# A fused attention and expert kernel on one core: one more token block by seven half-size products, another order of the first loads, another written-out order of the work

## The chip, the core and the metric

The kernel runs on one core of one Trainium2 chip. A core has five engines with queues of their own, each in order: TensorE (PE, the matrix products; its weight loads are listed apart as PEld), VectorE (DVE), ScalarE (ACT), GpSimd (POOL) and SyncE (SP). They wait for each other through semaphores. The metric is the device time of one execution in microseconds (us), the median of the runs.

## The reference

What is computed is an attention with a narrow window, and behind it two matrix products with a squared ReLU between them:

```python
# q, k, v: [8 batches, 8 heads, 576 positions, 64]
scores = q @ k.transpose(0, 1, 3, 2) / 8
scores = where(abs(pos[:, None] - pos[None, :]) <= 32, scores, -1e9)
attn = softmax(scores)
o = attn @ v
x = o.transpose(0, 2, 1, 3).reshape(8 * 576, 512)     # 4608 tokens of 512
h = x @ w_in                                          # 512 x 2048
r = maximum(h, 0.0)
g = r * r
out = g @ w_out                                       # 2048 x 512, float32
```

## The kernel before

**Attention.** The 8 x 576 queries are cut into 24 groups of 192, numbered G (batch `G // 3`, third `G % 3`). For a group the q, k and v rows are loaded; q and k are turned so that the head dimension lies on the partitions; a score step S (lines 600 and 609) multiplies them, an exponential X on ScalarE (627, 630) and, from the second batch on, a mask multiply M on VectorE (635) follow, then the product P with v (665), the reciprocal and the normalisation on VectorE (681, 684), and the turn T of the result into x transposed (`xt`). Most groups do this in two halves, A and B. P B of a group needs the upper half of its accumulator set to zero, which ScalarE does for most groups (656); the groups below `ZG` do without and write P B in 64-column tiles instead, twice as many matmuls.

The first three groups get their mask as a bias added by PE (`NPM = 3`, line 600). Groups of the first two batches are turned by PE (552, 701, 706) and copied out by ScalarE and VectorE (561, 564, 711); the later ones by transposing DMAs on the SP queue (572 for q and k, 715 and 718 for x).

**First product, x @ w_in.** It starts as soon as tokens are there. Up to token 4096 a piece of it, `mm1`, is some matmuls into one 512-wide bank (736: A), a ReLU out of that bank on ScalarE (742) and a square on VectorE (745). Pieces are 192 tokens wide below token 768, 256 below 2048, then 512. The tokens from `512 * MSTART` on take `mm1_strassen` instead. This computes the product of 2 x 2 blocks by seven products of half the size in place of eight, with sums of blocks of x (807, VectorE) and of w_in (792). One round handles a quarter of the hidden columns: 28 matmuls of 256 columns (835), two 512-wide products at a time in two banks, `x` and `y`. Between the seven products ScalarE copies a bank aside three times (842, "seed", `u` and `p`). Two of the four result blocks come straight from a bank (a ReLU on ScalarE, 861, a square on VectorE, 855); the other two are sums of a bank and a copy (`hb`, VectorE, 872), which a letter `ADDED` then sends on: "A" is a ReLU and a square on ScalarE (861, 853), "M" a ReLU on ScalarE and a multiply on VectorE (855), "D" one fused VectorE instruction that takes the maximum with zero and multiplies by the sum. One of the sums of w_in (`sums_w1(..., late=True)`) is written over a part of w_in that a plain `mm1` reads, so it comes behind the last plain piece.

**Second product, g @ w_out.** The first 512 tokens take plain matmuls (756), all others a seven-product form of their own (941 for the matmuls, 954 for copies, 912 for sums of g, 975 to 985 for the output). The last 512 tokens have a variant of it (`last`, 994 to 1024).

**The loads.** q, k and v are float32 in memory and are cast to bfloat16 on the way by DMAs issued from POOL (487 for q and k, 516 for v, 523 and 528 for 512 KB chunks of w_in and w_out). `load_hw` is the other way: a plain DMA issued by SP or ScalarE (503) into a float32 buffer and a cast on VectorE or ScalarE (505). The list `OPEN` gives the loads of the first batch, the engine of each, and a first order.

**What sets the order.** Nothing runs as it stands in the code. Each step is recorded with an estimated duration and a key, `Prog.schedule` simulates the five engines and the DMA queues by these estimates and always takes the ready step with the smallest key, and `emit` writes each engine's steps in the order so found, with waits where a step depends on another engine's. `ADJ` is a list of 1,143 numbers, one per step, added to the keys. Up to the first second-product step the planner fills gaps of PE with small matmuls on zeros (416). On the chip the order is fixed; a step that is late holds up all that stands behind it on its engine.

The kernel's other constants that the change touches: `SEP = (0,)` gives group 0 separate score banks, and `TB` does not exist yet: groups 0 to 2 are all turned in bank `outp0`.

Of the kernel before, what the change touches and what calls it, by code (L numbers as in the profile page):

```python
# [7 lines left out]
BF16 = mybir.dt.bfloat16  # L8
# [15 lines left out]
MSTART = 8  # L24
# [13 lines left out]
NSPLIT = 6  # L38
NXT = 6
DIRECT = "D"  # L40
ADDED = "A"
SEP = (0,)
ZG = 1
ADJ = dict(enumerate((
# [322 lines left out]
class Gen:  # L367
# [217 lines left out]
    def scores(self, G, ws):  # L585
        b, g = divmod(G, 3)
        i = b % 2
        kt, qt = self.KT[i], self.QT[i]
        key = 3 * G + OG[G] - LEAD + 0.3 * ws[0]
        a = 192 * g  # L590
        pm = G < NPM
        reg = {w: w if len(ws) == 2 or G in SEP else 0 for w in ws}

        def f(e):
            for w in ws:
# [561 lines left out]
```

## Time and profile before

| what | value |
|---|---|
| median of 3 runs | 299.95 us (298.72 to 300.38) |
| the profiled execution | 297.93 us |
| its span | 296.1 us, so 1.83 us lie around the span |
| PE busy | 288.8 us, 98% of the span |
| DVE, ACT, POOL busy | 200.4, 189.6, 118.8 us |
| granted clock of PE | full in each stage |

The page lists busy times by engine, the span in 40 slices, the DMA queues, the chain of work that ended last, the costliest groups of instructions, and the DMA issues. Further views of the same execution: the groups by line and shape with the mean duration of one instruction, the waits of one engine, the chain of waits in order of time, the timeline of a stretch, and tables of several windows. In a row of the timeline or of the chain the first number is the start in us, the second the duration, and in brackets stands a wait just before with what ended it. Matmuls are pipelined: the mean of a group is the time that one takes from start to end, and the time from one to the next is shorter; it is read from a run of them in the chain (its duration by its count).

### The profile page before, as it was taken

To read this page: it belongs to the slowest core of one execution; us is meant where nothing else is said; L and a number is where in the kernel's file an instruction comes from. 1 tells how busy PE (TensorE), PEld (TensorE's weight loads), DVE (VectorE), ACT (ScalarE), POOL (GpSimd) and SP (SyncE) were. 2 spreads that over 40 slices of the span, in tenths; PEclk is the share of its full clock that TensorE was granted. 3 is DMA by queue.
4 is the path that set the end of the run, shared out by engine and by line. 5 is a ranking of instruction groups with operands and counts; after the bars stand their busy time and mean duration, and the time that the engine had idled before them with its cause. 6 is when DMAs were issued, how large, how long until landed. Compare 5 with 4: busy or idle time off the path is not lost.

```text
span 296.1 us, 7502 instructions
## 1 busy us (share of the span) xinstructions
PE 288.8 (98%) x3027; PEld 223.2 (75%) x3027; DVE 200.4 (68%) x433; ACT 189.6 (64%) x305; POOL 118.8 (40%) x154
## 2 busy tenths in 40 slices
PE   8979999999989999999999999999999999999996
PEld 8758877767878888888655766775576556888885
DVE  6325894765597788767886964787785765872842
ACT  3556747877775667765677477455764776587740
POOL 8999576053592562970014679103900000000000
PEclk9999999999999999999999999999999999999999
DMA  9999999999999999999959999999997101121224
GB/s 141 129 194 199 204 157 174 172 145 133 163 175 135 163 175 153 171 171 164 184 95 126 106 201 145 148 178 172 157 134 150 46 18 28 37 73 38 71 74 142
DMA packets 179587, 40.26 MB, mean 136 GB/s; under 512 B 166752, under 2 KB 179040, under 8 KB 179552
## 3 DMA queue, kind: packets, MB, share of 16 engines
q0 software_dynamic: 122960, 19.11, 94.4%
q1 hardware_dynamic: 45984, 10.99, 30.7%
q10 hardware_dynamic: 10608, 9.67, 11.2%
q8 instruction: 24, 0.39, 0.6%
q14 instruction: 11, 0.09, 0.1%
HBM read 38.80 MB, written 9.44 MB: 163 GB/s over the span
## 4 chain that ended last, share of the span: by engine, by line
PE 80%; DMA 10%; POOL 7%; issue 1%; ACT 0%; DVE 0%; ACTq 0%; POOLq 0%
PE ps L736 33%; PE ps L941 27%; DMA kraw<-in_k_dram 6%; PE ps L756 5%; PE ps L835 4%; PE ps L609 4%; PE ps L665 4%; DMA w<-in_moe_w_in_dram 3%; POOL v L516 3%; POOL qraw L487 2%; POOL kraw L487 2%; DMA kt<-kraw 1%; PE ps L416 1%; PE ps L552 1%; PE ps L706 0%
## 5 line engine op out<-in xcount | busy, mean ns | idle before, releaser
L736 PE MATMUL ps<-xt,w 128*128 128x256 bf16 (+2 forms) x832 | 126.2, 298 | 1.3 <-DMA w<-in_moe_w_in_dram 1.3
L742 ACT ACTIVATE rt<-ps 128x512 bf16<-128x512 f32 (+1 forms) x136 | 76.7, 571 | 47.4 <-PE ps L736 37.9
L736 PEld LDWEIGHTS ps<-xt,w 128*128 128x128 bf16 x832 | 74.6, 98 | 29.9 <-DMA w<-in_moe_w_in_dram 1.5
L745 DVE TENSOR_TENSOR gt<-rt 128x512 bf16<-128x512 bf16 (+1 forms) x136 | 54.6, 404 | 30.5 <-ACT rt L742 28.4
L487 POOL DMA_DIRECT2D qraw<-in_q_dram x47 | 37.2, 810 | 75.6 <-PE ps L736 36.9
L941 PE MATMUL ps<-w,gt 128*128 128x256 bf16 x512 | 63.4, 273 | 0.0
L941 PEld LDWEIGHTS ps<-w,gt 128*128 128x128 bf16 x512 | 49.3, 98 | 8.1
L630 ACT ACTIVATE e<-ps 128x1024 bf16<-128x1024 f32 x42 | 41.4, 1021 | 3.9 <-PE ps L609 3.8
L516 POOL DMA_DIRECT2D v<-in_v_dram x48 | 42.1, 892 | 3.9 <-PE ps L609 3.8
L487 POOL DMA_DIRECT2D kraw<-in_k_dram x46 | 36.5, 810 | 15.7 <-PE ps L736 10.1
L635 DVE TENSOR_TENSOR pt<-e,mask 128x1024 bf16<-128x1024 bf16 x42 | 29.0, 691 | 14.3 <-ACT e L630 14.0
L941 PE MATMUL ps<-ts,ss 128*128 128x256 bf16 x256 | 32.0, 273 | 0.0
L941 PEld LDWEIGHTS ps<-ts,ss 128*128 128x128 bf16 x256 | 24.8, 98 | 4.7
L681 DVE RECIPROCAL rs<-ps 64x8 f32<-64x8 f32 (+1 forms) x48 | 10.0, 209 | 18.7 <-PE ps L665 17.8
L665 PEld LDWEIGHTS ps<-v,pt 128*128 128x128 bf16 (+1 forms) x400 | 18.1, 99 | 4.4 <-issue 1.2
L665 PE MATMUL ps<-v,pt 128*128 128x65 bf16 (+1 forms) x400 | 20.1, 194 | 1.0 <-ACT ps L656 1.0
L609 PEld LDWEIGHTS ps<-qt,kt 64*128 64x128 bf16 x384 | 10.8, 94 | 10.2 <-issue 9.2
L656 ACT ACTIVATE ps<-zz 64x520 f32<-64x520 bf16 x23 | 13.8, 599 | 7.0 <-DVE xa L684 6.0
L684 DVE TENSOR_TENSOR xa<-ps,rs 64x512 bf16<-64x512 f32 x24 | 16.7, 694 | 0.8
L684 DVE TENSOR_TENSOR xb<-ps,rs 128x512 bf16<-128x512 f32 x24 | 16.5, 688 | 0.7
L416 PE MATMUL ps<-zz 128*128 128x128 bf16 x180 | 15.6, 246 | 1.2 <-DVE zz L410 1.2
L912 DVE TENSOR_TENSOR gt<-gt,ss 128x1024 bf16<-128x1024 bf16 x16 | 10.6, 687 | 9.0 <-PE ps L941 8.9
(85 smaller groups left out, 278.6 us busy)
## 6 DMA issues: line engine op xcount, KB each, us to landing
out_dram<-oe ACTq DMA_DIRECT2D x34, 256.0 KB, 5.1
qraw<-in_q_dram POOLq DMA_DIRECT2D x47, 96.0 KB, 6.4
v<-in_v_dram POOLq DMA_DIRECT2D x32, 128.0 KB, 6.9
w<-in_moe_w_in_dram POOLq DMA_DIRECT2D x4, 512.0 KB, 10.2
w<-in_moe_w_out_dram POOLq DMA_DIRECT2D x4, 512.0 KB, 17.1
kraw<-in_k_dram POOLq DMA_DIRECT2D x15, 112.0 KB, 10.0
kraw<-in_k_dram POOLq DMA_DIRECT2D x16, 96.0 KB, 7.8
v<-in_v_dram POOLq DMA_DIRECT2D x16, 96.0 KB, 7.3
```

Source lines behind the costliest of these rows:

```text
L416: self.p.idle = lambda e: e.matmul(self.OUTP[1][:, 0:128], self.ZZ[:, 0:128], self.ZZ[:, 0:128], start=True, stop=True)
L487: self.p.rec("POOL", lambda e, j=j: e.dma_start(raw[0:h, j, :].rearrange("p (h d) -> p h d", h=8), s[:, j]), writes=[("raw", t, G % NRAW, ...
L516: self.p.rec("POOL", lambda e, j=j, lo=lo, hi=hi, k0=k0: e.dma_start(vt[lo - k0:hi - k0, j, :, 0:64], self.v[b, :, lo:hi, :].rearrange("h ...
L609: mm = e.matmul(sc[:, 512 * par + 128 * j:512 * par + 128 * j + 128], kt[r:r + 64, j, k0:k0 + 128], q, start=not pm, stop=True, skip_group ...
L630: self.p.rec("ACT", lambda e, e_=e_, sc=sc: e.activation(e_[:], sc, ACTF.Exp, scale=0.125), reads=tags[w], writes=[("e", n % 2)], key=key, ...
L635: self.p.rec("DVE", lambda e, pt=pt, ee=ee, mb=mb: e.tensor_tensor(pt[:], ee, mb, ALU.mult), reads=[("e", n % 2), ("mask", mi)], writes=[( ...
L665: mm = e.matmul(avp[z:z + n, cc:cc + 65], pt[:, 4 * (h % 2) + h // 2, z:z + n], vt[:, w, h, 0:65], start=((w == 0 or z == 64) and y == 0), ...
L684: self.p.rec("DVE", lambda e: e.tensor_tensor(x[r0:128, :].rearrange("p (x y c) -> p x y c", x=2, y=4), av[:, :, :, 0:64], rb, ALU.mult), ...
L736: mm = e.matmul(ht[:, n * x:n * x + n], self.W1[:, ft, 128 * d:128 * d + 128], self.XT[:, ft, r:r + n], start=(ft == 0), stop=(ft == 3))
L742: self.p.rec("ACT", lambda e: e.activation(rt[:, 0:c], ht[:, 0:c], ACTF.Relu), reads=[f"ht{k % 2}"], writes=[("rt", k % 4)], key=key, dur= ...
L745: self.p.rec("DVE", lambda e: e.tensor_tensor(gt[:, d0:d0 + len(ds), rg:rg + n], rr, rr, ALU.mult), reads=[("rt", k % 4)], writes=[("gt", ...
L941: mm = e.matmul(op[:, 256 * y:256 * y + 256], lhs[:, l0[0] + k, a:a + 128], rhs[:, r0 + k, c0:c0 + 256], start=start and y == 0 and k == 0 ...
```

## The change

`MSTART` goes from 8 to 7: tokens 3584 to 4095 too are computed by `mm1_strassen`, so the sums of w_in with the late one among them, and a matmul that sets a bank's bits, now stand ahead of token 3584. `ADDED` becomes a string with one letter for each round: "D" for the four rounds of tokens 3584 to 4095, "M" for the four of tokens 4096 to 4607 (it was "A" for all). `ZG` goes from 1 to 2, so that group 1's P B is written in tiles, 16 matmuls for 8, without a zero fill. With `TB = 1` group 0 is turned in bank `ht0`. `FLIP = ()`, the `divmod` in the loads and the test with `any` change nothing here. `OPEN` has another order, and both k halves of group 0 come by SP with a cast on VectorE each (before: one of them); no load goes by ScalarE any more (before: two). All numbers of `ADJ` are new.

```diff
-MSTART = 8
+MSTART = 7
...
-ADDED = "A"
+ADDED = 'DDDDDDDDDDDDDDDDDDDDDDDDDDDDDDDDMMMM'
 SEP = (0,)
-ZG = 1
+ZG = 2
+TB = 1
+FLIP = ()
...
-OPEN = [("k", 0, 0, "POOL"), ("q", 0, 1, "POOL"), ("q", 2, 0, "POOL"), ("k", 0, 1, "SP"), ("q", 0, 0, "POOL"), ("v", 1, 1, "POOL"),
-        ("v", 0, 0, "POOL"), ("v", 0, 1, "POOL"), ("k", 1, 1, "POOL"), ("k", 2, 1, "ACT"), ("v", 1, 0, "POOL"), ("q", 1, 0, "POOL"),
...
+OPEN = [('k', 0, 0, 'SP'), ('k', 0, 1, 'SP'), ('q', 0, 0, 'POOL'), ('q', 0, 1, 'POOL'), ('k', 1, 0, 'POOL'), ('k', 1, 1, 'POOL'),
...
         if G < NXT:
             ps, bank = self.AT[:, 1024:1536].bitcast(BF16), self.half(2)
-            if G < 3:
+            if G < TB:
+                ps, bank = self.HT[0][:].bitcast(BF16), ["ht0"]
+            elif G < 3:
                 ps, bank = self.OUTP[0][:].bitcast(BF16), ["outp0"]
...
-            if ADDED != "D":
-                square(i, j, *relu(hb[:], [("hb", n % 2)], k), k, ADDED)
+            how = ADDED[t0 // 128 + d // 2]
+            if how != "D":
+                square(i, j, *relu(hb[:], [("hb", n % 2)], k), k, how)
                 return
```

After the planner, POOL's first loads stand in this order (batch 0; behind the letter the group and the half):

```
before: q0.1 q0.0 k0.0 [iota] k1.1 v0.1 v0.0 v1.1 q2.0 v1.0 q1.0 k1.0 q1.1 w_in(0) v2.0 w_in(1) w_in(2) k2.0 w_in(3) v2.1
after:  [iota] q0.0 q0.1 k1.0 k1.1 v0.0 w_in(2) v1.0 v0.1 q1.1 q1.0 v1.1 q2.0 q2.1 k2.0 w_in(0) w_in(1) k2.1 v2.0 w_in(3) v2.1
```

The iota is the small POOL instruction from which the masks are made (424).

Later in the program the two k halves of group 20 stand six loads earlier in POOL's queue than before.

More of the change, by code (lines that the diff above doesn't have):

```diff
@@ L40 @@
 DIRECT = "D"
-ADDED = "A"
+ADDED = 'DDDDDDDDDDDDDDDDDDDDDDDDDDDDDDDDMMMM'
 SEP = (0,)
-ZG = 1
+ZG = 2
+TB = 1
+FLIP = ()
 ADJ = dict(enumerate((
[98 rows of a table removed]
-OWN = (0,)
-OPEN = [("k", 0, 0, "POOL"), ("q", 0, 1, "POOL"), ("q", 2, 0, "POOL"), ("k", 0, 1, "SP"), ("q", 0, 0, "POOL"), ("v", 1, 1, "POOL"),
[4 rows of a table removed]
[100 rows of a table added]
+OWN = (0,)
+OPEN = [('k', 0, 0, 'SP'), ('k', 0, 1, 'SP'), ('q', 0, 0, 'POOL'), ('q', 0, 1, 'POOL'), ('k', 1, 0, 'POOL'), ('k', 1, 1, 'POOL'), ('v', 0, 0, 'POOL'), ('v', 0, 1, 'POOL'), ('q', 1, 0, 'POOL'), ('q', 1, 1, 'POOL'), ('v', 1, 0, 'POOL'), ('v', 1, 1, 'POOL'), ('w1', 0, 0, 'POOL'), ('w1', 1, 0, 'POOL'), ('w1', 2, 0, 'POOL'), ('k', 2, 0, 'POOL'), ('k', 2, 1, 'POOL'), ('q', 2, 0, 'POOL'), ('q', 2, 1, 'POOL'), ('w1', 3, 0, 'POOL'), ('v', 2, 0, 'POOL'), ('v', 2, 1, 'POOL'), ('w2', 0, 0, 'POOL'), ('w2', 1, 0, 'POOL'), ('w2', 2, 0, 'POOL'), ('w2', 3, 0, 'POOL')]
 NPM = 3
@@ L591, in scores @@
         pm = G < NPM
-        reg = {w: w if len(ws) == 2 or G in SEP else 0 for w in ws}
+        reg = {w: w if len(ws) == 2 or G in SEP else 1 if G in FLIP else 0 for w in ws}
         def f(e):
@@ L642, in pv @@
         key = 3 * G + OG[G] - LEAD + 0.3 * w + 0.1
-        reg = 1 if G < NSPLIT and G not in SEP else 0
+        reg = 1 if G < NSPLIT and G not in SEP + FLIP else 0
         c0 = 1024 * reg
@@ L1056, in build @@
             key = K + n
+            b, g = divmod(a, 3)
             if t == "w1":
@@ L1061, in build @@
             elif t == "v":
-                self.load_v(0, a, key, (j,))
+                self.load_v(b, g, key, (j,))
             elif eng != "POOL":
@@ L1065, in build @@
             else:
-                self.load_qk(t, 0, a, key, (j,))
+                self.load_qk(t, b, g, key, (j,))
         todo = []
@@ L1074, in build @@
             base, turn = 3 * G - 9, 0.6 if b < NTURN else 3
-            if b:
+            if not any(it[:2] == ("v", G) for it in OPEN):
                 key = 3 * G + OL[G] - LEAD - AHEAD
```

201 rows, old and new, of tables (ADJ, OPEN) are left out of this document.

## The prediction

> **What bounds the kernel now.** I read the busy line and the chain first, then a table of windows, PE's waits, and last the chain in order of time.
>
> ```profile
> span 296.1 us, 7502 instructions
> PE 288.8 (98%) x3027; PEld 223.2 (75%) x3027; DVE 200.4 (68%) x433; ACT 189.6 (64%) x305; POOL 118.8 (40%) x154
> PE 80%; DMA 10%; POOL 7%; issue 1%; ACT 0%; DVE 0%; ACTq 0%; POOLq 0%
> ```
>
> The window rows give, behind the window and its length, busy time and count of PE, PEld, DVE, ACT and POOL, then PE's granted clock; the windows are the opening, the stretch to the token 3584 pieces, these pieces (with second products among them), the token 4096 rounds, and the tail. Two more rows are the same view for the planner's idle matmuls (416) alone.
>
> ```profile
> 0.00:28.88 28.88, 25.57 (x381) 21.72 (x381) 13.11 (x53) 14.17 (x20) 27.71 (x40) 1.00 1.52 164
> 28.88:219.30 190.42, 189.02 (x2010) 144.07 (x2007) 140.85 (x292) 128.02 (x202) 91.05 (x116) 1.00 1.78 159
> 219.30:245.80 26.50, 26.50 (x218) 16.06 (x216) 17.49 (x37) 17.90 (x30) 0.00 (x0) 1.00 0.45 74
> 245.80:275.80 30.00, 30.00 (x265) 25.72 (x264) 18.98 (x36) 21.04 (x39) 0.00 (x0) 1.00 0.16 49
> 275.80:296.10 20.30, 17.73 (x163) 15.64 (x160) 9.94 (x18) 8.44 (x17) 0.00 (x0) 1.00 0.28 92
> ...
> 0.00:28.88 28.88, 14.55 (x171) 12.33 (x171) 1.00 1.52 164
> 28.88:296.10 267.22, 1.00 (x9) 0.61 (x9) 1.00 1.35 133
> ```
>
> PE is busy without a gap from 219.3 to 275.8 us, and all but 1.4 of 190.42 us before that; its clock is full throughout. Only the opening is loose: 14.55 of its 25.57 busy us are idle matmuls. So there are two places to gain: less PE work anywhere behind 28.9 us, and an earlier end of the opening. PE's waits say how little else there is:
>
> ```profile
> PE ps L736 <- DMA w<-in_moe_w_in_dram: 1.3, 1, 1.3
> PE ps L665 <- ACT ps L656: 1.0, 1, 1.0
> PE ps L609 <- DMA kt<-kraw: 0.4, 1, 0.4
> ```
>
> The first belongs to the opening; behind it only a zero fill (group 7's P B) and group 20's turned k end waits. The sum below is made against the profiled execution, 296.1 of span and 1.83 around it, 297.93; that is 2.02 below the median, and I add this back at the end.
>
> **1. Tokens 3584 to 4095: 64 matmuls of 512 columns become 112 of 256.** In the chain an uninterrupted run of each stands as
>
> ```profile
> 142.53 1.73 PE ps L736 x8
> 255.10 3.06 PE ps L835 x28
> ```
>
> 1.73/8 = 0.216 us and 3.06/28 = 0.109 us: half the width takes half the time. 64 x 0.216 = 13.84; 4 rounds x 28 x 0.109 = 12.24 with the rounded row (3.06 x 4). PE loses **1.6 us**, and since PE waits for nothing there, the end moves by as much, if the round's helpers keep up. The matmul that sets a bank's bits moves with the stage and stays one.
>
> The trace also says what would make this fail. A round needs 28 weight loads:
>
> ```profile
> L835 PEld LDWEIGHTS ps<-xt,w 128*128 128x128 bf16 x32 | 3.1, 98 | 1.0
> ```
>
> 98 ns lie under a matmul of 109 with 11 to spare. The saving is gone if each half-size matmul took 13.84/112 = 123.5 ns. The Trainium skill, "TensorE: Matmul & The Clock Gate", section "Back-to-back issue gap", gives some 131 ns for a sustained matmul of 512 columns with its weight load and some 81 for one of 128; on the line between them a matmul of 256 takes an estimated 98, and 64 x 131 = 8.4 us would become 112 x 98 = 11.0, a loss of 2.6. The rows disagree: 216 and 109 are in the ratio 2.
>
> The helpers of a round, before (the last letter's way) and after:
>
> ```profile
> L842 ACT ACTIVATE uf<-ps 128x512 f32<-128x512 f32 x8 | 4.7, 593 | 2.2 <-DVE hb L872 1.2 <-PE ps L835 1.0
> L861 ACT ACTIVATE rt<-ps 128x512 bf16<-128x512 f32 x8 | 4.8, 595 | 1.9 <-DVE gt L855 1.0 <-DVE gt L912 0.7 <-PE ps L835 0.2
> L872 DVE TENSOR_TENSOR hb<-ps,uf 128x512 bf16<-128x512 f32 x8 | 5.4, 688 | 3.7 <-ACT rt L861 2.2 <-PE ps L941 0.7 <-ACT uf L842 0.4
> L855 DVE TENSOR_TENSOR gt<-rt 128x512 bf16<-128x512 bf16 x8 | 3.4, 420 | 2.5 <-ACT rt L861 2.4
> L853 ACT ACTIVATE gt<-rt 128x512 bf16<-128x512 bf16 x8 | 4.9, 625 | 0.4 <-PE ps L941 0.4
> L742 ACT ACTIVATE rt<-ps 128x512 bf16<-128x512 f32 x104 | 61.0, 596 | 38.1 <-PE ps L736 31.7 <-PE ps L665 2.4 <-DVE ss L912 1.6
> L745 DVE TENSOR_TENSOR gt<-rt 128x512 bf16<-128x512 bf16 x104 | 43.4, 419 | 22.2 <-ACT rt L742 20.5 <-PE ps L941 0.5
> ```
>
> At 3584 the 16 pieces gave ScalarE 16 x 0.596 = 9.5 and VectorE 16 x 0.419 = 6.7. Four rounds now give ScalarE 12 copies and 8 ReLUs, 20 x 0.594 = 11.9, and VectorE 4 sums of x (0.42 each, as the nearest bfloat16 row), 8 `hb` (0.688), 8 squares (0.42) and 8 fused maximum-multiplies. The fused one is unseen at this size: it lies between 0.42 (a bfloat16 multiply) and 0.69 (a sum from a bank); I take the upper end, as no row shows a fused form at the multiply's speed. Sum 1.7 + 5.5 + 3.4 + 5.5 = 16.1, which is 9.4 more than before. "M" at 4096 moves 8 squares: ScalarE less 8 x 0.625 = 5.0, VectorE 8 x 0.42 = 3.4 more. VectorE had 17.49 + 18.98 = 36.5 us in the 56.5 of the two windows; with 9.4 and 3.4 it has 49.2 in some 54.9, **90%**. ScalarE has 38.9 + 11.9 - 9.5 - 5.0 = 36.3. This still fits, but the slack is thin: a round uses two banks in turn, a product behind a bank waits for its copy, `hb` or ReLU, and VectorE's queue is 90% full. Second products between (941) cover it; without them a round (3.1 us of PE) has 16.1/4 = 4.0 us of VectorE work. I put **+0.3** for one or two short waits, with bounds 0 and +2.5 (16.1 - 12.24 = 3.9 of VectorE work beyond the rounds' own PE time, of which the second products among them cover at least a part).
>
> **2. Group 1's P B in tiles.** Sixteen matmuls of 64 columns for eight, and no zero fill on ScalarE. The rows at 12.06 (under 3) and 80.40 (under 4) give 0.45 for sixteen and 0.42 for eight, so the price lies between 0.03 and, if twice as many cost twice as much, 0.42: **+0.1** for PE, near the first, which is the same form.
>
> **3. The opening.** Before, in order of time:
>
> ```profile
> 3.84 0.26 POOL L424 IOTA dif<- 128x128 f32 x1
> 6.71 0.42 DVE L505 CAST kraw<-oe 112x512 bf16<-112x512 f32 x1
> 12.06 0.45 PE L665 MATMUL ps<-v,pt 128*64 128x65 bf16 x16
> 19.25 1.50 PE L736 MATMUL ps<-xt,w 128*128 128x192 bf16 x16 [1.29 <-DMA w<-in_moe_w_in_dram]
> 28.89 1.49 PE L736 MATMUL ps<-xt,w 128*128 128x192 bf16 x16
> ```
>
> The first two w_in chunks issued landed after 7.6 and 9.3 us (issue to landing):
>
> ```profile
> w<-in_moe_w_in_dram POOLq DMA_DIRECT2D x1, 512.0 KB, 7.6
> ...
> w<-in_moe_w_in_dram POOLq DMA_DIRECT2D x1, 512.0 KB, 9.3
> ```
>
> The chain after, by hand, each load at the spacing of before's landings. The iota first puts every load back by 0.26 and makes the masks some 2.5 us earlier, which nothing was waiting for. Two casts on VectorE instead of one end at about 7.5; scores A of group 0 start at about 8.9, as before. One cost is known from POOL's issues (shortest, mean, longest):
>
> ```profile
> L516 POOL DMA_DIRECT2D v<-in_v_dram x16: 774/905/1245, 4.8 to 48.1; - x16
> L516 POOL DMA_DIRECT2D v<-in_v_dram x2: 774/1010/1245, 5.7 to 6.5; - x2
> ```
>
> The only issue of 1245 ns is the one that lies over the cast at 6.71, 0.34 above the mean; two casts cost the queue **+0.35** more. (The Trainium skill, "SBUF — State Buffer", section "SBUF: two separate sides", names this: VectorE's copies within SBUF in float32 keep POOL's DMA descriptors from being written. The row agrees.) Chunk 2 of w_in now stands sixth, ahead of group 0's second v half, whose P B so runs at 13.5 to 15 instead of 12.06; group 1's q lands at 14.0 to 16.2, chunk 0 at 19.2 to 21.5 (before, just ahead of 19.25). The first mm1 starts at 20.5 to 22 in place of 19.25, but finds more work ready: turns of groups 0 to 2 and four pieces then run with no idle matmuls between. The point to compare is the start at 28.89, by which six first-product pieces, group 2's scores A, two turns of x and all turns of the first batch were done. Adding up PE's work from the first mm1 on gives 27.1 for the early landings, 27.5 to 28.1 for the middle ones, 28.6 for the late ones, to which the cast adds up to 0.7. I take 28.1: **-0.8**, bounds -1.8 and +0.7. Eight idle matmuls behind this point against nine are no change.
>
> **4. Group 7's zero fill.**
>
> ```profile
> 80.40 0.42 PE L665 MATMUL ps<-v,pt 128*128 128x65 bf16 x8
> 81.72 0.60 ACT L975 ACTIVATE oe<-ps 128x512 f32<-128x512 f32 x1 [0.84 <-PE ps L941]
> 82.79 0.60 ACT L656 ACTIVATE ps<-zz 64x520 f32<-64x520 bf16 x1 [0.47 <-ACT oe L975]
> 83.54 0.41 PE L665 MATMUL ps<-v,pt 128*128 128x65 bf16 x8 [0.98 <-ACT ps L656]
> ```
>
> P B waits 0.98 because the fill stands behind an output copy on ScalarE. In the new order 2.0 us of PE work lie between the halves as before, but the output copy is elsewhere and the fill should end some 0.3 earlier: **-0.3**, bounds -1.0 and +0.5 (such a wait in another group).
>
> **5. Group 20's scores.** The chain holds this as its one transfer late in the program:
>
> ```profile
> 185.55 17.03 DMA kraw<-in_k_dram
> 202.59 3.60 DMA kt<-kraw
> 206.33 0.62 PE ps L609 x16
> ```
>
> The scores stood at 206.33 after the 0.4 wait above and a gap. In the new order they stand some 4 us of PE work earlier, so turned k is needed at about 202. Its raw k is issued six loads earlier in POOL's queue; the transfers land one behind the other, so it should land at 190 to 194, and the last transposes then sit behind group 18's `xb` in SP's order, issued near 195 and landed near 202. A wait of 0 to 1 replaces one of 0.4 to 0.6: **0**, bounds -0.6 and, if raw k lands as late as before, +4.2.
>
> **The sum.** -1.6 + 0.3 + 0.1 - 0.8 - 0.3 + 0 = **-2.3**: span 293.8, profiled time 295.6, and by the 2.02 between the profiled run and the median 297.65, say **297.6**.
>
> **The rivals.** A change under 0.5% (1.5 us) can't be told from none here.
>
> *The opening comes late.* Chunk 0 waits behind fourteen loads and chunk 2 has taken bandwidth ahead of it; the late end of term 3 (+0.7 in place of -0.8) or a first mm1 beyond 22 us leaves some -0.5 in all: 299.5. For it speaks that the queue is full (DMA share over 1.5 in the window), against it that the same bytes are moved.
>
> *VectorE becomes the bound at 3584.* At 90% load, with waits of its bound +2.5: 299.8. For it: `hb` already had waits of ScalarE and PE before it; against it: the second products can stand between.
>
> *Group 20's turned k is late, the rival on the slower side.* If transposes land at 206.2 in spite of the earlier raw loads, PE waits 4.2 at 202, and 297.6 + 4.2 = 301.8. It cancels the gain from a landing at 204.3 on and makes it slower by 0.5% from 206 on. For it: transposes issue in SP's order behind group 18's, which depend on PE; against it: six places in the queue.
>
> *Half-size matmuls cost more than half* in this place. If a third of each weight load (98/3 = 33 ns) weren't hidden, 112 x (0.109 + 0.033) = 15.9 us would stand for 13.84: +2.1 instead of -1.6, 301.3. The run of 28 at 0.109 speaks against it.
>
> **How the numbers follow.** Forecast 0.55 (its own range 296 to 298.6); opening late 0.20; VectorE 0.12; group 20 0.11; half-size 0.02. The range goes down to the low bounds of terms 3, 4, 5 and 1 together, 297.6 - 1.0 - 0.7 - 0.6 - 0.3 = 295.0, and up to group 20's full price, 301.8; some 0.13 lies above it or below. Faster by over 0.5% (below 298.45) is the forecast with 0.02 from the milder ends of the opening and VectorE cases, 0.57; within, most of those two, 0.25; slower, group 20, half-size and 0.05 of those two at their worst, 0.18.
>
> **What would show it.** Right: L835's line with 224 matmuls at 0.109 in runs of 28, 64 fewer of 512 columns at the first product, no wait of PE between 219 and 275; first mm1 near 21, group 2's scores A done near 28; a tail as before. Wrong: a wait of PE for `kt` near 202, waits for `hb` or the banks in the 3584 rounds, a first mm1 beyond 22, or a new ScalarE wait at a P B in place of group 7's.

## The result, and the profile after

| | median | lowest to highest | runs |
|---|---|---|---|
| before | 298.9 us | 296.84 to 302.02 | 17 |
| changed | 296.88 us | 296.25 to 299.07 | 17 |

The ratio is 0.9944, 95% interval 0.9918 to 0.997. That is 1.7 us or 0.56% faster, inside the range of 295.0 to 301.8 and in the direction forecast; the sum had given 2.3. Two later measurements of the changed kernel, each on another chip beside its own runs of before, gave 1.0004 (0.9971 to 1.0037) and 0.9966 (0.9934 to 0.9999). The plain mean of the three ratios is 0.9971, so 0.9 us.

Part of the spread between them has a visible source. In 3 of 17, 7 of 12 and 5 of 12 executions of the changed kernel the mean granted clock of PE was lowered, to 0.994 or 0.993 of full speed, and these executions took 1.4 to 1.9 us longer than the others (the last section has more on it). The ratios leave out executions over 1.5% above the fastest of the same kernel, which on the second chip takes out 8 of the 9 lowered-clock executions of before, and none of the changed kernel's 7. Of those that enter the ratios, the ones at full clock (0.999 or 1.00) have means of 297.86 against 298.79 us there, a ratio of 0.997 from only five executions of the changed kernel, and of 296.90 against 298.38 us on the third chip, 0.995. So the level result of the second chip comes in good part from the clock. The kernel is faster, by 0.3 to 0.6%; the experiments below show what moves it. (The list `ADJ` has 1,433 numbers before and 1,459 after, one per step, not 1,143 as the description of the kernel has it; nothing was worked out from that.)

The page of the changed kernel, its busy line and its chain:

```profile
span 295.0 us, 7629 instructions
PE 287.5 (97%) x3082; PEld 227.8 (77%) x3082; DVE 210.9 (71%) x454; ACT 185.5 (63%) x298; POOL 119.1 (40%) x155
PE 88%; DMA 5%; ACT 2%; POOL 2%; issue 1%; DVE 1%; ACTq 0%; POOLq 0%; SPq 0%
```

The windows: the opening, the stretch to the half-size rounds, both blocks of rounds, the tail (busy time of PE, PEld, DVE, ACT, POOL, then the clock):

```profile
0.00:27.69 27.69, 25.18 (x390) 21.56 (x390) 12.90 (x53) 12.25 (x17) 26.73 (x39) 1.00 1.57 163
27.69:217.40 189.71, 187.31 (x1982) 141.53 (x1979) 139.37 (x289) 128.55 (x202) 92.33 (x117) 1.00 1.73 157
217.40:275.00 57.60, 57.60 (x563) 49.38 (x560) 48.27 (x95) 38.24 (x67) 0.00 (x0) 1.00 0.47 70
275.00:295.00 20.00, 17.42 (x160) 15.37 (x157) 10.34 (x20) 6.51 (x13) 0.00 (x0) 1.00 0.28 93
```

The third row is the main reading: with VectorE at 48.27 of 57.60 us (84%), PE is busy for 57.60 of 57.60. No helper of the half-size rounds holds it up. The second row has the bad news: PE's gap is 189.71 - 187.31 = 2.4 us, where before it was 190.42 - 189.02 = 1.4. PE's waits name what is new:

```profile
PE ps L609 <- DVE gt L747: 1.0, 1, 1.0
PE ps L665 <- DMA v<-in_v_dram: 1.0, 1, 1.0
PE ps L665 <- ACT ps L656: 0.5, 1, 0.5
PE ps L609 <- DMA qt<-qraw: 0.4, 1, 0.4
PE ps L738 <- ACT rt L744: 0.2, 1, 0.2
```

The wait for the first w_in chunk (1.3) is gone, one for v (1.0) has come; behind the opening stand waits of 1.0 and 0.4 at scores and 0.2 at a first product, while group 7's fill went from 1.0 to 0.5 and group 20's wait is gone. The named VectorE square is not what the first of these waited for. That score step is group 15's, and its last q transpose, issued at 141.47 the moment the raw q landed, landed itself at 150.26:

```profile
140.23 2.48 SPq L572 DMA_TRANSPOSE qt<-qraw  x2
...
150.35 0.62 PE L609 MATMUL ps<-qt,kt 64*128 64x128 bf16 x16 [1.01 <-DVE gt L747]
```

In the opening, by the timeline:

```profile
10.75 0.45 PE L665 MATMUL ps<-v,pt 128*64 128x65 bf16 x16
14.42 0.45 PE L665 MATMUL ps<-v,pt 128*64 128x65 bf16 x16 [1.00 <-DMA v<-in_v_dram]
21.10 0.82 PE L738 MATMUL ps<-xt,w 128*128 128x192 bf16 x8
27.36 0.40 PE L609 MATMUL ps<-qt,kt 64*128 64x128 bf16 x8
```

Group 2's scores A start at 27.36, with the same six pieces of the first product behind them as at 28.56 before: 1.2 us earlier. From that point to the end of the span, before and after:

```profile
28.56:296.10 267.54, 263.57 (x2655) 201.70 (x2654) 187.59 (x381) 175.40 (x285) 91.37 (x116) 1.00 1.35 133
27.36:295.00 267.64, 262.66 (x2702) 206.50 (x2701) 198.04 (x402) 173.54 (x282) 92.66 (x117) 1.00 1.35 134
```

For this one pair of executions the account is: 1.2 us earlier out of the opening, and behind it nothing, since PE's busy time is 0.9 us less and its idle time 1.0 us more (3.97 to 4.98). This makes the 1.1 between the spans of 296.1 and 295.0. The half-size products alone should have taken 1.6 off the busy time; where the other 0.7 went is not shown.

### The profile page after: what moved, and what is told of

Same layout as the page of the kernel before. It is cut to its first block, busy times and chain, and to the rows that moved or that the text cites. A ratio compares the mean times of both kernels' runs of the same rounds, so it can differ in the third digit from the quotient of the medians.

```text
span 295.0 us, 7629 instructions
## 1 busy us (share of the span) xinstructions
PE 287.5 (97%) x3082; PEld 227.8 (77%) x3082; DVE 210.9 (71%) x454; ACT 185.5 (63%) x298; POOL 119.1 (40%) x155
## 4 chain that ended last, share of the span: by engine, by line
PE 88%; DMA 5%; ACT 2%; POOL 2%; issue 1%; DVE 1%; ACTq 0%; POOLq 0%; SPq 0%
PE ps L944 32%; PE ps L738 31%; PE ps L837 8%; PE ps L758 5%; PE ps L609 4%; PE ps L665 4%; DMA qt<-qraw 3%; DMA v<-in_v_dram 2%; PE ps L416 2%; ACT e L630 1%; PE ps L552 1%; ACT rt L744 1%; PE ps L600 1%; POOL qraw L487 1%; PE ps L708 1%
## 5 line engine op out<-in xcount | busy, mean ns | idle before, releaser
L738 PE MATMUL ps<-xt,w 128*128 128x256 bf16 (+2 forms) x768 | 109.5, 290 | 0.4 <-ACT rt L744 0.2
L744 ACT ACTIVATE rt<-ps 128x512 bf16<-128x512 f32 (+1 forms) x120 | 67.0, 567 | 40.4 <-PE ps L738 30.6
L738 PEld LDWEIGHTS ps<-xt,w 128*128 128x128 bf16 x768 | 69.0, 98 | 22.2 <-ACT rt L744 0.6
L747 DVE TENSOR_TENSOR gt<-rt 128x512 bf16<-128x512 bf16 (+1 forms) x120 | 47.5, 403 | 22.7 <-ACT rt L744 20.3
L487 POOL DMA_DIRECT2D qraw<-in_q_dram x48 | 38.8, 821 | 50.5 <-PE ps L738 48.5
L609 PE MATMUL ps<-qt,kt 64*128 64x128 bf16 x384 | 15.9, 218 | 1.6 <-DVE gt L747 1.0
L656 ACT ACTIVATE ps<-zz 64x520 f32<-64x520 bf16 x22 | 13.2, 600 | 6.4 <-DVE xa L684 6.2
L944 PE MATMUL ps<-ts,gt 128*128 128x256 bf16 x128 | 16.0, 273 | 0.0
```

The costliest lines, as they stand in the source:

```text
L487: self.p.rec("POOL", lambda e, j=j: e.dma_start(raw[0:h, j, :].rearrange("p (h d) -> p h d", h=8), s[:, j]), writes=[("raw", t, G % NRAW, ...
L609: mm = e.matmul(sc[:, 512 * par + 128 * j:512 * par + 128 * j + 128], kt[r:r + 64, j, k0:k0 + 128], q, start=not pm, stop=True, skip_group ...
L738: mm = e.matmul(ht[:, n * x:n * x + n], self.W1[:, ft, 128 * d:128 * d + 128], self.XT[:, ft, r:r + n], start=(ft == 0), stop=(ft == 3))
L744: self.p.rec("ACT", lambda e: e.activation(rt[:, 0:c], ht[:, 0:c], ACTF.Relu), reads=[f"ht{k % 2}"], writes=[("rt", k % 4)], key=key, dur= ...
L747: self.p.rec("DVE", lambda e: e.tensor_tensor(gt[:, d0:d0 + len(ds), rg:rg + n], rr, rr, ALU.mult), reads=[("rt", k % 4)], writes=[("gt", ...
L944: mm = e.matmul(op[:, 256 * y:256 * y + 256], lhs[:, l0[0] + k, a:a + 128], rhs[:, r0 + k, c0:c0 + 256], start=start and y == 0 and k == 0 ...
```

## The experiments

In the experiments each engine's order is written out as a list, so that only the steps named move. Ratios are to the kernel before, run beside them on the same chip.

| run | ratio | 95% interval |
|---|---|---|
| changed kernel, second chip | 1.0004 | 0.9971 to 1.0037 |
| changed, 3584 plain again (same chip) | 1.006 | 1.0017 to 1.0103 |
| before with the new opening (same chip) | 1.0027 | 0.9992 to 1.0063 |
| changed, five steps moved (same chip) | 0.9988 | 0.9951 to 1.0026 |
| before itself, third chip | 1.0003 | 0.9969 to 1.0038 |
| changed kernel (same chip) | 0.9966 | 0.9934 to 0.9999 |
| changed, more VectorE work (same chip) | 1.0006 | 0.9971 to 1.0041 |
| changed, third w_in chunk later (same chip) | 0.9928 | 0.9892 to 0.9964 |
| before with the half-size rounds alone, fourth chip | 0.9941 | 0.991 to 0.9972 |
| before with the opening and the later chunk (same chip) | 0.9987 | 0.9963 to 1.0011 |
| changed, group 20's k six loads later (same chip) | 1.0109 | 1.0072 to 1.0146 |
| best version (same chip) | 0.9907 | 0.9877 to 0.9937 |

### The half-size products, taken out and put in alone

Out of the changed kernel:

```diff
-MSTART = 7
+MSTART = 8
 # 16 plain pieces stand where the 28 half-size products stood, the last sum of w_in behind them
```

> The changed kernel itself, with its order written out as a list in place of the planner (each engine's instructions are the same), as the measure for the three runs beside it. Every theory expects the ratio of the changed kernel, 0.994, so some 1.5 to 2 us under the kernel before.

> The changed kernel with tokens 3584 to 4095 by 64 plain matmuls of 512 columns again, everything else in the same order. My theory (the saving on PE is 64 x 0.216 - 112 x 0.109 = 1.6 us and no helper eats it): 1.6 us slower than the changed kernel, about the time of before, PE without a wait in the stage in both. Rival (the helpers of the half-size rounds take some of it back): under 0.8 us slower. Rival (the gain of the change is in the opening alone): no slower.

Into the kernel before, up to group 21's scores as it was, and from there in the changed order:

```diff
-MSTART = 8
+MSTART = 7
-ADDED = "A"
+ADDED = 'DDDDDDDDDDDDDDDDDDDDDDDDDDDDDDDDMMMM'
```

> The kernel before up to group 21's scores, in its own order and with its own opening, then the changed kernel's order with tokens 3584 to 4095 by half-size products. Theory (64 x 0.216 - 112 x 0.109 = 1.6 us less on PE, VectorE at 84% there still hides its part): 1.2 to 1.8 us faster than before. Rival (the gain of the changed kernel is its opening): within 0.5 us of before.

Taking them out cost 1.006 - 1.0004 = 0.56%, 1.7 us; putting them in alone gained 0.59%, 1.8 us. The theory had 1.6. Each alone is uncertain by some 0.3 to 0.5%, but they agree from two sides, at full clock alone too (299.82 against 297.86 us and 297.15 against 298.83, so 2.0 and 1.7), and the rival that all the gain lies in the opening falls. In a single profile the first pair says less than it seems: of the 1.8 us between their spans (296.4 and 298.2) some 0.9 came from the opening, which waited 2.1 us for v in the one and 1.3 in the other.

### How much room VectorE has

```diff
             p.rec("DVE", lambda e: e.scalar_tensor_tensor(dst, ss, 0.0, ss, ALU.max, ALU.mult), ...)
+            p.rec("DVE", lambda e: e.scalar_tensor_tensor(dst, ss, 0.0, ss, ALU.max, ALU.mult), ...)   # once more
```

> The changed kernel with each of the eight fused VectorE instructions of tokens 3584 to 4095 issued twice: 8 x 0.685 = 5.5 us more VectorE work where the prediction reckoned VectorE at 90% (measured 48.3 of 57.6 us, 84%). Prediction's reading (the slack is thin, the second products cover some of it): 0.5 to 2 us slower, PE waits for hb or a bank in the stage. Rival (the order by which the products follow leaves each round so much room that VectorE has slack all through): within 0.3 us, no wait.

It was 0.4% slower than the changed kernel beside it (1.0006 against 0.9966, so 1.2 us, with intervals that overlap; at full clock the means are 298.90 and 296.90). The trace is clearer. In the stage, by the window and the timeline:

```profile
217.40:275.00 57.60, 56.22 (x545) 47.19 (x547) 52.10 (x101) 36.53 (x64) 0.00 (x0) 1.00 0.45 70
```

```profile
238.14 0.62 PE L609 MATMUL ps<-qt,kt 64*128 64x128 bf16 x16 [0.34 <-DVE xb L684]
246.52 0.43 PE L665 MATMUL ps<-v,pt 128*128 128x65 bf16 x8 [0.45 <-DVE pt L635]
262.11 1.92 PE L837 MATMUL ps<-xs,ws 128*128 128x256 bf16 x16 [0.43 <-DVE xs L809]
```

VectorE at 52.10 of 57.60 (90%) makes PE wait three times, 1.2 us in all; at 84% it did not. From the first half-size product to the last it took 56.9 us, against 55.0 and 55.3 in two traces of the changed kernel. The prediction's reading that the slack is thin holds; only the load had been put too high, at 49.2 of 54.9. Note who waits: attention steps and the sums of x, queued behind the squares, more than the rounds' own banks.

### The opening

The changed opening alone, joined to the kernel before behind 31 us:

```diff
-OPEN = (before's)
+OPEN = (the changed kernel's), ZG = 2, TB = 1; steps up to 31 us in the changed kernel's order
```

> The kernel before with the changed kernel's opening alone (order of loads, both k halves by SP, bank of group 0's turn, tiles for group 1), and behind 31 us its own order. My theory after comparing the traces (the opening is worth some 1.2 us: PE's wait of 1.3 for the first w_in chunk goes, a wait of 1.0 for v comes where PE has filler to lose): faster than before by 0.8 to 1.4 us, no wait for w_in in PE's list. Rival (what the opening gains is lost at the next transfers, since the bytes are the same and land no earlier): within 0.4 us of before.

The change in the other direction, one load moved within the changed kernel:

```diff
 POOL: iota q0.0 q0.1 k1.0 k1.1 v0.0
-w_in(2) v1.0 v0.1 q1.1 ... k2.0 w_in(0) w_in(1) k2.1
+v1.0 v0.1 q1.1 ... k2.0 w_in(0) w_in(1) w_in(2) k2.1
```

> The kernel before once more, for its trace on the chip of the runs beside it. On the last chip the changed kernel was level with it (1.0004), where the first measurement had 0.994. If the opening is what moves between chips, its scores A of group 2 start within 0.5 us of 28.6, as in its first trace, while those of the changed kernel move between 27.4 and 28.7 with the landing of group 0's second v half.

> The changed kernel (order written out) once more on the same chip. Theory (PE work less by 1.5 us, the opening by 0 to 1.3 as v lands, 1.5 us of new waits for transfers): ratio to before between 0.994 and 1.000, waits of PE behind 30 us some 1.5 us more than before's. Rival (the first measurement was right and the last chip disturbed): 0.994 again.

> The changed kernel with the third w_in chunk moved in POOL's queue from the sixth place to behind the second chunk; nothing else moves. Theory (the opening hangs on group 0's second v half, which the 512 KB ahead of it hold up by some 2.5 us, and all behind it is a chain): that v lands near 12 instead of 14.3, group 0's P B starts near 12.2 instead of 14.4, group 2's scores A near 25.5 instead of 27.4 to 28.7, and the time falls by 1.5 to 2.5 us against the changed kernel. Rival (the opening hangs on the sum of the bytes, so that the chunk is then late itself): scores A of group 2 stay at 27 or later, time within 0.5 us.

The repeat of before gave the 28.6 expected, within 0.3 us, and the repeat of the changed kernel the ratio expected; its waits behind 30 us came to 1.97 us against 1.46 in before beside it, so 0.5 more and not 1.5.

The first opening alone gained nothing (1.0027), and the wait for v explains most of it. That wait was 1.00 us in the first trace of the changed kernel, 1.34 in the second, 2.56 in the third, 1.85 in this join, and group 2's scores A followed it: they started at 27.36, 27.77, 28.90 and 29.73 (the last one with a lowered clock on top, which the section on the hardware shows). Four more executions of the changed opening fit: waits of 1.00 and 2.09 with starts at 27.27 and 28.66, and 1.65 and 1.66 with 28.69 and 28.76, these two with another wait of some 0.5 us for a w_in chunk. In before they started at 28.56 and 28.89. So the changed opening is 1.2 us ahead in one execution and level in another, by the landing of one load. (The join also waited 0.31 and 0.83 us for transposes at 202 and 208, where before had 0.42, and 8 of its 12 executions had the lowered clock.) In the third execution the timeline has

```profile
10.75 0.45 PE L665 MATMUL ps<-v,pt 128*64 128x65 bf16 x16
15.97 0.45 PE L665 MATMUL ps<-v,pt 128*64 128x65 bf16 x16 [2.56 <-DMA v<-in_v_dram]
```

and with the chunk moved (same chip)

```profile
10.87 0.45 PE L665 MATMUL ps<-v,pt 128*64 128x65 bf16 x16
13.47 0.45 PE L665 MATMUL ps<-v,pt 128*64 128x65 bf16 x16
25.09 0.45 PE L552 MATMUL ps<-ident,kraw 80*128 80x80 bf16 x8 [0.67 <-DMA kraw<-in_k_dram]
28.40 1.49 PE L738 MATMUL ps<-xt,w 128*128 128x192 bf16 x16 [0.39 <-DMA w<-in_moe_w_in_dram]
```

The wait is gone and P B stands right behind the filler matmuls; the time fell by 0.38% against the changed kernel beside it, 1.1 us of the 1.5 to 2.5 expected. At full clock the means differ by only 0.35 us (296.55 and 296.90); the larger part is that none of the 10 executions had the lowered clock, where 5 of 12 had it beside them. V itself landed at 10.74, but P B could not start before 13.47, behind the fillers. The rest of the lead went into the last two rows: group 2's second k half and the last w_in chunk are now what is late, so group 2's scores A started at 27.23, not at 25.5. Both theories were partly right: v hung on the chunk, and behind it the sum of the bytes is near.

The same later chunk in the join with the kernel before:

```diff
 (the join above)
-w_in(2) in sixth place
+w_in(2) behind w_in(1)
```

> The kernel before with the changed kernel's opening and, as in the run before, the third w_in chunk behind the second. Theory (what decides the opening is whether v of group 0 stands behind a 512 KB chunk): no wait of PE for v, 1.0 to 1.8 us faster than before, and at least 1.5 us faster than the same join with the chunk in sixth place (ratio 1.0027 there). Rival (the join itself costs, whatever v does): still within 0.4 us of before.

It gained 0.4% on the first join (1.0027 to 0.9987, on another chip), with no lowered clock in 12 executions where the first join had 8. Against before it gained only 0.13%, where at least 1.0 us was expected: the time is the rival's. PE had no wait for v, as expected, and its opening did run ahead (scores A of group 2 at 27.45, where three executions with before's opening have 28.32 to 28.89). It was given back at 200 us:

```profile
201.32 1.67 PE L736 MATMUL ps<-xt,w 128*128 128x512 bf16 x7 [1.07 <-DMA xt<-xb]
...
207.51 0.62 PE L607 MATMUL ps<-qt,kt 64*128 64x128 bf16 x16 [0.79 <-DMA kt<-kraw]
```

Before reached this score step at 206.33 with a wait of 0.42; here it runs at 207.51. (The run with the half-size rounds alone, on the same chip and in before's order up to here, has it at 207.10 after a wait of 0.80.) Group 20's raw k landed at 202.56 and 203.61, behind the same loads as before. A lead gained early ends at the next transfer that doesn't come earlier, and this is where the changed kernel's later order pays: it has these two loads ahead.

### Group 20's k

```diff
 POOL: ... q20.1 q20.0
-k20.1 k20.0 v21.1 v21.0 q21.1 q21.0 k21.1 k21.0
+v21.1 v21.0 q21.1 q21.0 k21.1 k21.0 k20.1 k20.0
```

The loads that go first are the six of group 21, its k too; the expectation's "four" counts them wrongly.

> The changed kernel with group 20's two k loads put back by four loads in POOL's queue, where the next group's v and q went first in the kernel before. The prediction's rival said that a late k costs what its transpose lands behind the time of need (up to 4.2 us). Theory: raw k lands near 196 to 198 in place of 189.5, its transposes near 203.5 to 205 in place of 201.3, and PE waits 0.5 to 2 us for kt near 203, where it waits for nothing now; the time goes up by as much. Rival (SP's queue, not the load, sets when the transposes land): no wait, time unchanged.

1.0109, against 0.9971 as the mean of the changed kernel: 1.4%, some 4 us, twice the upper end expected. In 8 of its 10 executions the clock was lowered; the two at full clock have a mean of 299.91 us, against 298.83 for before, which puts them 2.0 to 2.6 us above the changed kernel's 0.995 to 0.997. So the wait seen below makes about half of it, and the clock the rest. On PE:

```profile
201.44 0.42 PE L665 MATMUL ps<-v,pt 128*128 128x65 bf16 x8
204.30 3.52 PE L738 MATMUL ps<-xt,w 128*128 128x512 bf16 x8 [2.45 <-DMA xt<-xb]
207.76 0.62 PE L609 MATMUL ps<-qt,kt 64*128 64x128 bf16 x16
```

It is not the scores that wait, but a first product, for group 18's turned x. SP's queue says why:

```profile
190.95 1.26 SPq L717 DMA_TRANSPOSE xt<-xa  x1
200.55 1.18 SPq L572 DMA_TRANSPOSE kt<-kraw  x1
201.83 1.22 SPq L720 DMA_TRANSPOSE xt<-xb  x1
203.10 1.24 SPq L572 DMA_TRANSPOSE kt<-kraw  x1
```

The k transpose stands in front and waits for its load; behind it the x transpose, which is ready, goes out at 201.83 where the changed kernel has it at 194.54. And the eight matmuls after the wait take 3.52 us in place of 1.9. The clock tells that:

```profile
201.50:204.00 2.50, 0.35 (x9) 0.23 (x7) 1.92 (x4) 0.60 (x1) 0.00 (x0) 1.00 0.43 86
204.00:205.00 1.00, 0.70 (x2) 0.28 (x3) 0.00 (x0) 0.00 (x0) 0.00 (x0) 0.61 0.40 82
205.00:206.00 1.00, 1.00 (x4) 0.32 (x3) 0.00 (x0) 0.00 (x0) 0.00 (x0) 0.50 0.32 59
207.00:208.00 1.00, 1.00 (x13) 0.24 (x12) 0.89 (x2) 0.14 (x1) 0.00 (x0) 0.69 0.47 93
208.00:209.00 1.00, 1.00 (x18) 0.54 (x13) 0.51 (x2) 1.00 (x2) 0.00 (x0) 1.00 0.52 109
```

### Taking the new waits away, and the best version

```diff
 POOL: v16.1 v16.0 behind q15.1 (before: ahead of group 15's v and k)
 SP:   the second half of q14's transpose ahead of group 12's x transpose
 DVE:  group 7's first normalisation ahead of a square
 ACT:  group 7's zero fill ahead of a ReLU
```

> The changed kernel with five steps moved: group 16's v loads behind group 15's q loads, one half of group 14's q transpose ahead of group 12's x transpose on SP, and, for group 7, the normalisation ahead of a square on VectorE and the zero fill ahead of a ReLU on ScalarE. My theory (three new waits of PE, 0.4 at 138, 1.0 at 150 and 0.5 at 82 us, are each held up by what stands ahead in one queue): these three waits go or fall under 0.2 each, and the time falls by 1 to 1.8 us. Rival (PE only waits later, since the next groups' transfers are as late): other waits of the same sum appear within 20 us, time within 0.4 us of the changed kernel.

```diff
 (the five moves above, and in POOL's opening)
-w_in(2) sixth ... k2.0 w_in(0) w_in(1) k2.1 v2.0 w_in(3)
+k2.0 w_in(0) w_in(1) k2.1 w_in(2) w_in(3) v2.0
```

> The changed kernel with the third w_in chunk behind the second as before, group 2's second k half ahead of it, the fourth chunk right behind it, and the five moves that took three waits of PE away. Theory (the rest of the opening now waits for those two loads, 0.7 and 0.4 us): group 2's scores A near 26.5, and 0.5 to 1.2 us below the run with the one move (ratio 0.9928), so a ratio of 0.988 to 0.991. Rival (PE's later waits come back elsewhere, as two of them did when they were moved): 0.993.

With the five moves alone the waits at 138 and 150 us went, but others came, as the rival said: 0.96 at a first product, ended by an output copy on ScalarE, and 0.53 next to group 7. The first of these is not new, though: in two executions of the changed kernel without the moves, the same product waited 0.61 and 0.77. By time nothing can be told (0.9988 beside 1.0004).

```profile
84.35 1.91 PE L738 MATMUL ps<-xt,w 128*128 128x256 bf16 x16 [0.53 <-issue]
...
143.10 1.89 PE L738 MATMUL ps<-xt,w 128*128 128x512 bf16 x8 [0.96 <-ACT oe L988]
```

The best version, with the opening's loads in the order of need, has a ratio of 0.9907, with medians of 295.95 and 299.13 us: by the ratio 2.8 us faster than before, and the fastest of all. None of its 9 executions had the lowered clock. It was expected at 0.988 to 0.991. Its group 2 scores A start at 26.55, and PE waits for no load at all. Against the changed kernel's mean of 0.9971 that is 0.6%; against the run with one load moved (0.9928, on another chip) the intervals overlap. It joins the five moves and the changes in the opening, and no run tells their shares apart.

## Why the prediction was right, and where not

The direction and the range held, and so did the first term. That the sum came near was in part luck, as the paragraph behind the list shows. By its steps:

1. *Half-size products, -1.6.* Right: 1.7 and 1.8 us from two sides, and half the width took half the time: in the chain of the changed kernel, 2.18/20 = 0.109 us each. The rival by the weight load falls.

```profile
259.67 2.18 PE ps L837 x20
```

The +0.3 for helpers was not there: PE had no wait in 57.60 us. The fused instruction took 0.69, the upper end that was chosen:

```profile
L882 DVE SCALAR_TENSOR_TENSOR gt<-hb 128x512 bf16<-128x512 bf16 x8 | 5.2, 685 | 0.0
```

2. *Tiles, +0.1.* Too small to be seen apart.
3. *The opening, -0.8 with bounds -1.8 and +0.7.* The size was right for the first trace (-1.2), but the step missed what decides it. P B of group 0 was put at 13.5 to 15 and taken as harmless, because work ready later would fill the gap. It was not: fillers are a fixed number of instructions in the queue, and whatever v's lateness is goes through to the end of the opening. P B stood at 14.35 to 15.97, and so the term is -1.2 to +0.3 against before's 28.56, from one execution to the next. The 0.35 for a second cast didn't come. Of the two casts the second lies over two issues of v:

```profile
6.11 1.78 POOL L516 DMA_DIRECT2D v<-in_v_dram  x2
...
6.75 0.51 DVE L505 CAST kraw<-oe 112x512 bf16<-112x512 f32 x1
```

These took 0.89 each, like the mean of before. The slow issue of before (1245 ns) was no accident, since it took 1244 ns in two more executions with that opening. But the cast is not enough to make it: of the four issues that the two casts now touch, none took over 0.91 us. What else delayed it stays open. The rule of the Trainium skill that was cited for it ("SBUF — State Buffer", section "SBUF: two separate sides") did not show here in either cast; the cast itself took 0.51 and 0.65 us where it had taken 0.42.

4. *Group 7's fill, -0.3.* The wait fell by 0.5, from 0.98 to 0.47, within the bounds.
5. *Group 20's scores, 0.* Right: the last transpose of its q and k landed at 202.65 and PE didn't wait, so the 0.4 of before is gone. Its rival came near in price by luck (4.2 reckoned, some 4 measured when the loads were put back): a wait of 2.45 us is about half of it and the lowered clock the rest, and what waited was not the scores but the step behind the waiting transpose on SP's queue.

What failed is a term that isn't in the sum: the new waits. The prediction asked only at group 7 and group 20 what becomes late when PE runs ahead, and took the other groups' transfers to be on time. In the first trace groups 14 and 15 had theirs late by 0.4 and 1.0 us, in the stretch where raw loads took 11 to 14 us from issue to landing. There the new waits come to 1.7 us (0.25 at a first product at 80 us, 0.43 and 1.01 at the scores), in the two later ones of the changed kernel to 2.5 and 1.5. Against them four terms did better than forecast: the helpers by 0.3, the opening by 0.4, the fill by 0.2, group 20 by 0.4. With these sizes the sum is -1.9 for the first pair, where the spans differ by 1.1; the other 0.8 is not assigned.

What stays open: why v of the same opening lands between 14.22 and 15.84 us. It is not the chip alone, for both ends were seen on the third one (15.84 in the changed kernel, 14.22 in the run with more VectorE work, which is the same up to the half-size rounds).

## What to carry to other kernels

When PE is the bound by a few percent, less PE work is a gain only as far as the next transfer comes earlier too: go along the in-order queues and ask, for each load that lands just in time, what it does when its user comes a microsecond sooner. In an opening, a large load ahead of a small one that is on the chain holds it up: here v landed at 14.2 to 15.8 us behind the 512 KB chunk and at 10.2 to 10.7 without it, and PE lost 1.0 to 2.6 us of that. Filler instructions of a fixed number pass every delay on. And a load that is late holds up what stands behind its transpose in the queue, before it holds up its own user.

## What the runs showed of the hardware

A wait of PE can cost more than its length. After 2.45 us without work, the granted clock went to 0.50 for some 3 us (the window rows under group 20's k), and eight matmuls of 512 columns took 3.52 us. The same happened once in an opening, after 1.85 us of waiting for v, in the join of the kernel before with the changed opening:

```profile
13.50:15.30 1.80, 0.05 (x3) 0.08 (x5) 0.00 (x0) 0.00 (x0) 1.80 (x3) 1.00 2.43 151
16.00:17.00 1.00, 1.00 (x17) 1.00 (x15) 0.67 (x1) 0.00 (x0) 1.00 (x2) 0.63 2.00 177
17.00:18.00 1.00, 1.00 (x14) 1.00 (x12) 0.00 (x0) 0.45 (x1) 1.00 (x3) 0.50 1.57 193
20.00:21.00 1.00, 1.00 (x24) 0.90 (x24) 0.00 (x0) 0.58 (x1) 1.00 (x3) 1.00 1.24 214
```

It is not certain to happen: after waits of 2.56, 2.09, 1.66 and 1.65 us for v in four other openings the clock stayed at 1.00. The Trainium skill, "TensorE: Matmul & The Clock Gate", section "HAM oscillation — how this bites in real kernels", warns of idle gaps above some 3.4 us; here the clock fell after gaps of 1.85 and 2.45, in two of these six cases.

Over all runs on record, the mean clock of an execution was 0.994 or less in 47 of 99 executions of the versions with the third w_in chunk in sixth place (waits for v of 1.00 to 2.56 us in their traces), in 26 of 127 with before's opening (a wait of 1.3 to 1.4 us for w_in in the two traces of before), and in none of 31 with the chunk moved back (no wait over 1.1 us in their three traces once PE has started). The chips don't explain it: on the third one it was 10 of 24 with the chunk in sixth place and 0 of 10 with it moved, on the fourth 8 of 10 (with the further wait at 204 us) and 0 of 21. Only two of the lowered-clock executions were traced, so that the others lost their clock at the same places is likely, not shown. So a wait of 2 us is to be priced at 2 us, or at up to 4, by chance.
